# A two-stage MoE kernel on one core: the next unit's first group moved between the last six products of a unit, and the PSUM banks dealt anew

## The chip, the cores and the metric

The kernel runs on one core of one Trainium2 chip. What counts is the device time of one execution in microseconds (us), less is better. Before the change the median of three runs is 2382.3 us (2381.95 to 2382.96).

## The reference, cut to what matters

```python
def _moe2_ref(x, w_gate, w1, w2):          # x (3072, 384): output of attention and a first MoE
    P = np.exp(logits - logits.max())      # logits = x @ w_gate
    for _ in range(8):                     # Sinkhorn
        P /= P.sum(1, keepdims=True) + 1e-09
        P /= P.sum(0, keepdims=True) + 1e-09
        P *= N / E
    for e in range(8):
        h = np.maximum(x @ w1[e], 0.0)     # w1[e] (384, 1024)
        out += P[:, e:e + 1] * (h @ w2[e]) # w2[e] (1024, 384)
```

A delta-rule attention and a first MoE layer come before this; they take the first 947 us or so of the execution and the change doesn't touch them.

## The kernel before, in words

The second MoE is worked off in 24 **units** (e, p): expert e of 8 on the token block p of 3, which is 1024 tokens. Every fp32 product is made of three fp16 matmuls (high by high, high by low, low by high), and both layers use a scheme with seven block products in place of eight.

A unit has two parts. First come four **groups** (class Group, line 1025), k = 0 to 3, for 256 of the 1024 hidden features each. A group has 11 terms, each of three matmuls 128x512 on TensorE (`prod`, L1040). They run in five PSUM banks that the class calls x, y, z, w and v: (0,0) starts in bank x, and its partial sum is copied by ScalarE to banks y, w and z at three places (`fork`, line 1048), where the sum grows on in other directions. From the finished banks ScalarE (`take`) and VectorE (`plus_v`) read c00, c01, c10, c11 and v, and of these come the seven operands of the second layer, A11, A12, A22, S1, S2, S3, S4. Each is rounded to fp16 by ScalarE (`hi`, L1012) and its rest subtracted by VectorE (`lo`, `lo_max`, L1015 and L1018). In the trace they are the tiles h{k}{n}h and h{k}{n}l with n = 0 to 6 in that order: h36l is the low half of S4 of group 3. `head`, `body` and `tail` (lines 1076 to 1114) write a group's operations; S1 to S4 come in `tail`.

Then come four **pairs** (class Pair, line 1118), i = 0 to 3, for 2 x 128 of the block's token rows each. A pair has seven **products** (`product`, L1133) of 12 matmuls 128x192: product 1 reads A11, 2 reads A12, 4 A22, 5 S1, 6 S2, 7 S3 and 3 S4. After each VectorE adds the bank to the sum in SBUF (`put`, line 1155: the rows `acc<-ph` and `acc<-b`). Products 6 and 7 go on in the bank of product 1, product 3 in that of product 5, so 7 of a pair can't start before the put of its 6, nor 3 before the put of 5.

Nothing of this runs in the order in which it is written: `Plan.run` (line 76) deals the operations to the engines, TensorE's in the written order as far as they are ready by its own costs, those of the other engines by due times. The outcome is a fixed queue per engine, and each engine works its queue off in order. The unit loop (lines 1329 to 1378) writes the order: the groups (`head` of group k, `tail` of k - 1, `body` of k), product 1 of pair 0, the last `tail`, the rest of products 1, 2 and 4, and then pair after pair 6, 5, 7, 3 (in the units of expert 0 pair 3 has all its products last, for it shares a bank with pair 0). At the end of a unit come the loads of the next block's x (tiles xoh and xol, `dma`), the stores and loads of the sums, and the weights of coming groups (`weight1`, `weight2`): ScalarE scales and rounds, GpSimd subtracts. In the first two units of expert 0 x is not loaded but made on ScalarE and GpSimd (`operands`). `clear` (line 1321) is a matmul whose result nobody reads; it sets a bank's state so that later matmuls add to what a fork has written there.

## Time and profile before

| | |
|---|---|
| median of three runs | 2382.3 us |
| profiled execution, its own time | 2374.54 us |
| its span, first to last instruction | 2372.8 us, mean granted TensorE clock 0.959 |
| busy over the span: TensorE / VectorE / ScalarE / GpSimd | 2200.5 (93%) / 1702.5 (72%) / 1432.9 (60%) / 680.9 (29%) us |
| second MoE, first to last matmul | 947.2 to 2369.4 us |

The profiled execution is 7.8 us shorter than the median of the runs. A matmul's row gives a modelled end: a 128x192 matmul has a row of 0.25 us, though in a full stream the next one starts 0.083 us later, so rows overlap. "Idle" in brackets at the end of a row is the time in which the engine had no row open just before, and the arrow names the instruction that ended it.

### The profile page before, as it was taken

The page shows a single profiled execution, that of the slowest core. Times are in us where ns is not written, and L with a number is a line of the kernel's source. Part 1 is how long each engine was busy: PE and PEld are TensorE (multiplying, and loading weights), DVE is VectorE, ACT ScalarE, POOL GpSimd, SP SyncE. Part 2 cuts the span into 40 slices and gives each one's busy share as a digit, 9 for nine tenths or more (in the row PEclk, how much of TensorE's full clock was granted, in tenths as well). Part 3 has the DMA queues.
Part 4 walks back from the last instruction along what each step waited for, and adds up shares of the span by engine and source line. Part 5 has one row for each costly group of instructions (what it writes and reads, how often), then busy time and mean ns, then how long its engine had stood idle before and what let it go on. Part 6 is the DMA issues. An engine that isn't in the chain of part 4 may idle for free.

```text
span 2372.8 us, 43674 instructions
## 1 busy us (share of the span) xinstructions
PE 2200.5 (93%) x17324; PEld 1664.1 (70%) x17324; DVE 1702.5 (72%) x3304; ACT 1432.9 (60%) x2632; POOL 680.9 (29%) x748
## 2 busy tenths in 40 slices
PE   6788799999999988989999999999999999999999
PEld 5676677777777766666667677677677677677676
DVE  8567876848574254888677777777777777777777
ACT  6878757465655554666766655655655655656554
POOL 5444402132332254222411421321311312312100
PEclk7678999989999999999999999999999999999999
DMA  3354575545544353323323323323323333323221
GB/s 115 123 187 157 188 264 166 182 157 165 200 150 145 122 211 127 106 76 140 121 101 121 114 101 121 114 101 121 114 100 122 117 109 123 109 103 131 98 102 51
DMA packets 123453, 312.90 MB, mean 132 GB/s; under 512 B 14960, under 2 KB 66800, under 8 KB 117104
## 3 DMA queue, kind: packets, MB, share of 16 engines
q1 hardware_dynamic: 123248, 310.11, 38.2%
q8 instruction: 136, 2.23, 0.4%
q14 instruction: 69, 0.57, 0.1%
HBM read 247.84 MB, written 62.13 MB: 131 GB/s over the span
## 4 chain that ended last, share of the span: by engine, by line
PE 57%; DVE 8%; ACT 2%; POOL 2%; issue 1%; DMA 0%; SPq 0%; DVEq 0%; ACTq 0%; POOLq 0%
PE b L1040 18%; PE ph L1133 13%; PE ph L1040 10%; PE b L1133 10%; PE po L684 1%; PE ph L632 1%; DVE acc L1018 1%; DVE h26l L1015 1%; DVE h36l L1015 1%; DVE c L1018 1%; DVE h35l L1015 1%; DVE h16l L1015 1%; POOL stg L887 0%; DVE gxl L838 0%; POOL w1l L874 0%
## 5 line engine op out<-in xcount | busy, mean ns | idle before, releaser
L1015 POOL TENSOR_TENSOR stg<-stg 128x128 f32<-128x128 f32 (+2 forms) x240 | 157.4, 676 | 900.0 <-ACT stg L1012 896.0
L1040 PEld LDWEIGHTS <-w1h 128*128 128x128 f16 x2112 | 206.2, 98 | 241.6 <-issue 7.9
L1040 PE MATMUL b<-xoh,w1h 128*128 128x512 f16 x672 | 254.7, 379 | 0.0
L1040 PE MATMUL b<-xoh,w1l 128*128 128x512 f16 x672 | 254.7, 379 | 0.0
L1040 PE MATMUL b<-xol,w1h 128*128 128x512 f16 x672 | 254.7, 379 | 0.0
L684 PE MATMUL po<-gh,w 128*128 128x512 f32 (+1 forms) x600 | 221.2, 412 | 11.6 <-ACT gh L672 11.4
L1018 DVE SCALAR_TENSOR_TENSOR acc<-ph,pm,acc 128x192 f32<-128x192 f32 x315 | 134.8, 428 | 134.2 <-PE ph L1133 132.6
L1012 ACT ACTIVATE b<-ph 128x512 f32<-128x512 f32 x288 | 165.9, 584 | 72.6 <-PE ph L1040 66.7
L1040 PEld LDWEIGHTS <-w1l 128*128 128x128 f16 x1056 | 103.4, 98 | 124.6
L632 PE MATMUL ph<-x1h,w 128*128 128x512 f32 (+1 forms) x600 | 184.4, 414 | 4.9 <-DMA w<-wa_scratch 2.9
L1018 DVE SCALAR_TENSOR_TENSOR c<-b,v 128x512 f32<-128x512 f32 x96 | 66.1, 688 | 137.5 <-PE b L1040 131.6
L1012 ACT ACTIVATE v<-b 128x512 f32<-128x512 f32 x96 | 57.1, 595 | 173.6 <-PE b L1040 172.3
L670 DVE TENSOR_TENSOR leak<-leak,ph 128x512 f32<-128x512 f32 (+1 forms) x100 | 66.0, 660 | 117.6 <-ACT leak L669 115.0
L1040 PE MATMUL ph<-xoh,w1h 128*128 128x512 f16 x384 | 145.5, 379 | 4.2 <-ACT b L1012 4.2
L1040 PE MATMUL ph<-xoh,w1l 128*128 128x512 f16 x384 | 145.5, 379 | 0.0
L1040 PE MATMUL ph<-xol,w1h 128*128 128x512 f16 x384 | 145.5, 379 | 0.0
L684 PEld LDWEIGHTS po<-gh,w 128*128 128x128 f32 x600 | 117.3, 198 | 36.9 <-ACT gh L672 16.6
L1012 ACT ACTIVATE c<-b 128x512 f32<-128x512 f32 x192 | 114.3, 595 | 40.7 <-PE b L1040 39.9
L1015 DVE TENSOR_TENSOR c<-c,c 128x512 f32<-128x512 f32 x192 | 134.2, 705 | 1.4
L1018 DVE SCALAR_TENSOR_TENSOR c<-c,c 128x512 f32<-128x512 f32 x192 | 131.6, 698 | 2.0
L684 PE MATMUL po<-gl,w 128*128 128x512 f32 (+1 forms) x300 | 123.9, 414 | 9.5 <-POOL gl L674 6.0
L632 PEld LDWEIGHTS ph<-x1h,w 128*128 128x128 f32 x600 | 113.1, 201 | 27.3 <-DMA w<-wa_scratch 3.3
(433 smaller groups left out, 6924.1 us busy)
## 6 DMA issues: line engine op xcount, KB each, us to landing
w<-wa_scratch SPq DMA_DIRECT2D x100, 768.0 KB, 4.4
acc_scratch<-acc SPq DMA_DIRECT2D x84, 384.0 KB, 2.7
acc<-acc_scratch SPq DMA_DIRECT2D x84, 384.0 KB, 3.7
wraw<-wc SPq DMA_DIRECT2D x128, 192.0 KB, 3.3
stg<-wc SPq DMA_DIRECT2D x64, 384.0 KB, 8.7
xoh<-xo_scratch SPq DMA_DIRECT2D x21, 1152.0 KB, 5.1
xol<-xo_scratch SPq DMA_DIRECT2D x21, 1152.0 KB, 8.2
raw<-wa SPq DMA_DIRECT2D x48, 256.0 KB, 3.0
```

Source lines behind the costliest of these rows:

```text
L632: pe.matmul(out=ps, lhsT=wt[:, c * 128:(c + 1) * 128], rhs=xx[:, c], start=(n == 0), stop=(n == 3 * KD - 1))
L670: dve.tensor_tensor(out=g, in0=g, in1=ps, op=ALU.max)
L684: pe.matmul(out=po[c][:, cols], lhsT=wt[:, DM + c * 128:DM + (c + 1) * 128], rhs=xx, start=(i == 1 and m == 0), stop=(i == n and m == 2), ...
L1012: return vec("ACT", n, lambda e: e.activation(out=out, in_=src, func=func, scale=scale), reads, writes, **kw)
L1015: return vec(eng, n, lambda e: e.tensor_tensor(out=out, in0=a, in1=b, op=fn), reads, writes, **kw)
L1018: return vec("DVE", n, lambda e: e.scalar_tensor_tensor(out=out, in0=a, scalar=scalar, in1=b, op0=f0, op1=f1), reads, writes, **kw)
L1040: ordered(pe.matmul(out=banks[b], lhsT=w[:, a], rhs=x[:, c].rearrange("p s k -> p (s k)"), start=start, stop=i == 2 and (a, c) == terms[-1 ...
L1133: ordered(pe.matmul(out=banks[b][:, 0:HD], lhsT=xx[:, o:o + 128], rhs=wt[:, t], start=first and k == 0 and j == 0, stop=k == NK - 1 and j ...
```

## The change

Six things change in the second MoE. Group 0 of the next unit (`ahead`) is written between the last six products of the present one: its operations stand in `steps`, a generator that stops after each term, and one step is taken after each of these products. That holds for every unit that has a successor with loaded x, 21 of 24; units (0, 0) and (0, 1), whose successor's x is still being made, and the last one have none. Product 6 of all four pairs goes first, then 5, 7 and 3 interleaved over the pairs. Products 5 and 3 get a second bank (`y5`), so that two pairs can be under way. The groups' bank x alternates between 0 and 7 for all experts (before: 7 and 6, and 6 alone for expert 0), y is 1 in place of 2, and v of group 0 is 3. Expert 0's pairs take banks 3 and 4 for y, its pair 3 gets a bank of its own, and the Sinkhorn chain moves from bank 7 to 6; for that two more clears per unit of expert 0 are needed. The puts that begin a sum in expert 0 (`fresh`) move from VectorE to ScalarE. The loads of the next x are written ahead of the products.

```diff
@@ class Group
-                self.x, self.y, self.z, self.w, self.v = 7 - k % 2 if e else 6, 2, 3, 4, 5
+                self.x, self.y, self.z, self.w, self.v = k % 2 * 7, 1, 3, 4, 5 if k else 3
-            def head(self):
+            def steps(self):
                 self.prod(self.x, [(0, 0)])
                 self.fork(self.y)
-
-            def body(self):
+                yield
                 self.prod(self.v, [(7, 7)])
                 self.take("v", self.v)
+                yield
                 self.prod(self.x, [(6, 6)], False)
                 self.fork(self.w)
+                yield
...
@@ class Pair
-                self.x, self.y, self.z = (0, 1, 5, 7 if e else 0)[i], 6, 2
+                self.x, self.y, self.z = (0, 1, 5, 7)[i], 6 if e else 3 + i % 2, 2
+                self.y5 = (6, 2, 6, 2)[i] if e else (3, 4, 2, 2)[i]
-                b = {1: self.x, 6: self.x, 7: self.x, 5: self.y, 3: self.y, 2: self.z, 4: self.y}[n]
+                b = {1: self.x, 6: self.x, 7: self.x, 5: self.y5, 3: self.y5, 2: self.z, 4: self.y}[n]
...
-                    vec("DVE", n, lambda e: e.tensor_copy(out=o, in_=src), [("ps", b)], [("acc", blk)])
+                    copy(n, o, src, [("ps", b)], [("acc", blk)])
...
@@ unit loop
-            if e:
-                order = [(1, 1), (0, 2), (0, 4), (2, 1), (1, 2), (1, 4), (3, 1), (2, 2), (2, 4), (3, 2), (3, 4)]
-            else:
-                order = [(1, 1), (0, 2), (2, 1), (0, 4), (1, 2), (1, 4), (2, 2), (2, 4)]
-            for i, q in order:
-                x[i].product(q)
-            for i, q in [(i, q) for i in range(4 if e else 3) for q in (6, 5, 7, 3)]:
+            if nxt and not made:
+                for i in range(2):
+                    dma(128 * 9 * TB * 2, xo[i].rearrange("p j s k -> p (j s k)"), xo_dram[nxt[1], i],
+                        [("xod", nxt[1], i)], XO if i == 0 else [("xol",)])
+            for i, q in [(1, 1), (0, 2), (0, 4), (2, 1), (1, 2), (1, 4), (3, 1), (2, 2), (2, 4), (3, 2), (3, 4),
+                         (0, 6), (1, 6), (2, 6), (3, 6), (0, 5), (1, 5), (0, 7), (0, 3), (1, 7), (1, 3), (2, 5)]:
                 x[i].product(q)
...
-            if not e:
-                for q in (1, 2, 4, 6, 5, 7, 3):
-                    x[3].product(q)
-            if u + 1 < len(units):
-                clear(2, hb[0][A11][0][:, 0:128], hb[0][A11][0], [("h", 0, A11, 0)])
+            if e == 0:
+                for b in (3, 4):
+                    clear(b, hb[0][S1][0][:, 0:128], hb[0][S1][0], [("h", 0, S1, 0)])
+            if nxt and not made:
+                ahead = Group(*nxt, 0)
+                it = ahead.steps()
+                clear(1, hb[0][S1][0][:, 0:128], hb[0][S1][0], [("h", 0, S1, 0)])
+                next(it)
+            for i, q in ((3, 5), (2, 7), (2, 3), (3, 7), (3, 3)) if e else ((2, 7), (2, 3), (3, 5), (3, 7), (3, 3)):
+                x[i].product(q)
+                if ahead:
+                    next(it)
...
+            for _ in it if ahead else ():
+                pass
             store(e, p, 0)
```

The planner decides where all this ends up. Three places show it.

TensorE in unit (7, 0), at the start of product 7 of pair 0 (it reads h05, S3). Before, the last rows of product 5 (h33, bank ph_10349) stand ahead of it:

```order
L1133 LDWEIGHTS h33h_10318
L1133 MATMUL ph_10349<-w2h1_9564,h33h_10318 128x192
L1133 LDWEIGHTS h33l_10319
L1133 MATMUL ph_10349<-w2h1_9564,h33l_10319 128x192
L1133 LDWEIGHTS h33h_10318
L1133 MATMUL ph_10349<-w2l1_9565,h33h_10318 128x192
L1133 LDWEIGHTS h05h_10280
L1133 MATMUL b0_10343<-w2h4_9570,h05h_10280 128x192
```

Now, product 5 of pair 1 (bank b2_10345) and a term of the next unit's group 0, (7,7) in bank b3, stand ahead of it:

```order
L1139 LDWEIGHTS h33h_10318
L1139 MATMUL b2_10345<-w2l1_9565,h33h_10318 128x192
L1040 LDWEIGHTS w1h3_9558
L1040 MATMUL b3_10346<-xoh_9546,w1h3_9558 128x512
L1040 LDWEIGHTS w1h3_9558
L1040 MATMUL b3_10346<-xol_9547,w1h3_9558 128x512
L1040 LDWEIGHTS w1l3_9559
L1040 MATMUL b3_10346<-xoh_9546,w1l3_9559 128x512
L1139 LDWEIGHTS h05h_10280
L1139 MATMUL b0_10343<-w2h4_9570,h05h_10280 128x192
```

Product 7 of pair 0 was the 17th of its unit's 28 products (12 of kinds 1, 2 and 4, three 6 and one 5 stood ahead) and is now the 19th (12, then four 6 and two 5); in the units with p = 0 of experts 1 to 7 the term (7,7) stands ahead of it as well.

VectorE in the same unit, from h13l (low half of S1, group 1) to the put of product 6 of pair 0 (`acc<-b0`). Before:

```order
L1015 TENSOR_TENSOR h13l_10291<-c111_10336,h13h_10290 128x512
L1015 TENSOR_TENSOR h23l_10305<-c112_10337,h23h_10304 128x512
L1015 TENSOR_TENSOR h33l_10319<-c110_10335,h33h_10318 128x512
L1018 SCALAR_TENSOR_TENSOR acc_10261<-ph_10349,pm_10262,acc_10261 128x192
L1018 SCALAR_TENSOR_TENSOR c101_10333<-c101_10333,c001_10327 128x512
L1018 SCALAR_TENSOR_TENSOR c102_10334<-c102_10334,c002_10328 128x512
L1018 SCALAR_TENSOR_TENSOR c100_10332<-c100_10332,c000_10326 128x512
L1015 TENSOR_TENSOR h15l_10295<-c011_10330,h15h_10294 128x512
L1015 TENSOR_TENSOR h25l_10309<-c012_10331,h25h_10308 128x512
L1015 TENSOR_TENSOR h35l_10323<-c010_10329,h35h_10322 128x512
L1018 SCALAR_TENSOR_TENSOR acc_10261<-b0_10343,pm_10262,acc_10261 128x192
```

Now:

```order
L1015 TENSOR_TENSOR h13l_10291<-c111_10336,h13h_10290 128x512
L1015 TENSOR_TENSOR h23l_10305<-c112_10337,h23h_10304 128x512
L1015 TENSOR_TENSOR h33l_10319<-c110_10335,h33h_10318 128x512
L1018 SCALAR_TENSOR_TENSOR acc_10261<-ph_10349,pm_10262,acc_10261 128x192
L1018 SCALAR_TENSOR_TENSOR acc_10261<-b2_10345,pm_10262,acc_10261 128x192
L1018 SCALAR_TENSOR_TENSOR c101_10333<-c101_10333,c001_10327 128x512
L1018 SCALAR_TENSOR_TENSOR c102_10334<-c102_10334,c002_10328 128x512
L1018 SCALAR_TENSOR_TENSOR c100_10332<-c100_10332,c000_10326 128x512
L1015 TENSOR_TENSOR h15l_10295<-c011_10330,h15h_10294 128x512
L1015 TENSOR_TENSOR h25l_10309<-c012_10331,h25h_10308 128x512
L1015 TENSOR_TENSOR h35l_10323<-c010_10329,h35h_10322 128x512
L1018 SCALAR_TENSOR_TENSOR acc_10261<-b0_10343,pm_10262,acc_10261 128x192
```

VectorE's order here is the same but for one more put ahead of the sums of S4 (c101 to c100).

ScalarE at the end of unit (6, 2), behind h36h (S4 of group 3), where the weights of expert 7 are made (stg is the raw weight, w1h its rounded half; a 128x768 row of w1h reads what GpSimd has added up in stg). Before:

```order
L1012 ACTIVATE stg_10352<-stg_10352,scl_69 128x768
L1012 ACTIVATE w1h4_9560<-stg_10352 128x384
L1012 ACTIVATE stg_10353<-stg_10353,scl_69 128x768
L1012 ACTIVATE w1h0_9552<-stg_10353 128x384
L1012 ACTIVATE w1h4_9560<-stg_10352 128x768
L1012 ACTIVATE stg_10354<-stg_10354,scl_69 128x768
L1012 ACTIVATE w1h1_9554<-stg_10354 128x384
L1012 ACTIVATE stg_10351<-stg_10351,scl_69 128x768
L1012 ACTIVATE w1h0_9552<-stg_10353 128x768
L1012 ACTIVATE v0_10338<-b5_10348 128x512
L1012 ACTIVATE v1_10339<-b5_10348 128x512
```

Now:

```order
L1012 ACTIVATE w1h4_9560<-stg_10352 128x768
L1012 ACTIVATE stg_10354<-stg_10354,scl_69 128x768
L1012 ACTIVATE b1_10344<-b0_10343 128x512
L1012 ACTIVATE w1h1_9554<-stg_10354 128x384
L1012 ACTIVATE v0_10338<-b3_10346 128x512
L1012 ACTIVATE stg_10351<-stg_10351,scl_69 128x768
L1012 ACTIVATE w1h0_9552<-stg_10353 128x768
L1012 ACTIVATE b4_10347<-b0_10343 128x512
L1012 ACTIVATE c000_10326<-b1_10344 128x512
L1012 ACTIVATE h00h_10270<-c000_10326 128x512
L1012 ACTIVATE w1h1_9554<-stg_10354 128x768
L1012 ACTIVATE b3_10346<-b0_10343 128x512
```

The forks of the group ahead (b1, b4 and b3 from b0) now stand between the weight rows, with a row that reads GpSimd's sums ahead of each.

## Rows read from the trace of the kernel before

**Rows 1.** Table of stretches: start:end, length, busy us (instructions) per engine, clock, DMA.
```profile
947.00:2369.00 1422.00, 1374.57 (x11281) 986.78 (x11281) 1099.93 (x2000) 848.84 (x1486) 341.31 (x392) 0.99 0.31 109
1060.30:1063.70 3.40, 3.03 (x20) 2.78 (x20) 2.48 (x8) 1.67 (x3) 3.40 (x4) 0.50 0.00 0
2067.30:2070.70 3.40, 2.97 (x20) 2.74 (x19) 2.61 (x8) 1.31 (x2) 3.32 (x7) 0.50 0.00 0
```
**Rows 2.** Waits view, TensorE, 947 to 2372 us: us in total, times, longest.
```profile
PE ph L1133 <- DVE acc L1018: 17.6, 21, 1.0
PE b L1133 <- DVE acc L1018: 17.4, 8, 2.8
PE ph L1133 <- DVE acc L1164: 6.7, 4, 2.4
PE ph L1040 <- ACT b L1012: 4.2, 6, 1.0
```
**Rows 3.** Waits view, TensorE, 1318 to 2372 us (experts 2 to 7).
```profile
PE ph L1133 <- DVE acc L1018: 15.4, 18, 1.0
PE b L1133 <- DVE acc L1018: 13.1, 6, 2.4
```
**Rows 4.** Timeline, TensorE, unit (5, 0): start, length, instruction, idle before and releaser.
```profile
1871.98 0.25 PE L1133 MATMUL b<-w2h,h00h 128*128 128x192 f16 x1
...
1883.86 0.25 PE L1133 MATMUL b<-w2h,h04h 128*128 128x192 f16 x1
...
1890.42 0.24 PE L1133 MATMUL b<-w2h,h05h 128*128 128x192 f16 x1 [2.44 <-DVE acc L1018]
...
1892.55 0.24 PE L1133 MATMUL ph<-w2h,h06h 128*128 128x192 f16 x1 [0.98 <-DVE acc L1018]
```
**Rows 5.** Timeline, VectorE, the same unit.
```profile
1873.85 0.41 DVE L1018 SCALAR_TENSOR_TENSOR acc<-b,pm,acc 128x192 f32<-128x192 f32 x1
...
1889.36 0.68 DVE L1015 TENSOR_TENSOR h35l<-c,h35h 128x512 f16<-128x512 f32 x1
1889.96 0.41 DVE L1018 SCALAR_TENSOR_TENSOR acc<-b,pm,acc 128x192 f32<-128x192 f32 x1
```
**Rows 6.** Timeline, VectorE, unit (6, 0): its first operation, and h01l.
```profile
2026.06 0.69 DVE L1018 SCALAR_TENSOR_TENSOR c<-b,v 128x512 f32<-128x512 f32 x1 [5.49 <-PE b L1040]
...
2028.21 1.76 DVE L1018 SCALAR_TENSOR_TENSOR h01l<-c,h01h 128x512 f16<-128x512 f32 x1
```
**Rows 7.** Timeline, TensorE: the clears of two units in a row, and a term's first matmul.
```profile
1901.46 0.38 PE L1322 MATMUL b<-h00h 128*128 128x512 f16 x1
1901.67 0.38 PE L1040 MATMUL b<-xoh,w1h 128*128 128x512 f16 x1
...
1958.96 0.38 PE L1322 MATMUL b<-h00h 128*128 128x512 f16 x1
```
**Rows 8.** Timeline, unit (0, 0): ScalarE's scaling of the next x, GpSimd's first and last operations.
```profile
991.22 1.56 ACT L1012 ACTIVATE stg<-stg,scl 128x1536 f32<-128x1536 f32 x1
...
992.92 5.62 POOL L1015 TENSOR_TENSOR stg<-stg 128x256 f32<-128x256 f32 x6 [70.55 <-ACT stg L1012]
...
1004.17 5.59 POOL L1015 TENSOR_TENSOR xol<-stg,xoh 128x256 f16<-128x256 f32 x4
```
**Rows 9.** DMA issues, 1985 to 2015 us: KB each, us from issue to landing.
```profile
xol<-xo_scratch SPq DMA_DIRECT2D x1, 1152.0 KB, 8.9
```
**Rows 10.** Timeline, ScalarE, expert 5: weight rows that waited for GpSimd.
```profile
1894.23 0.84 ACT L1012 ACTIVATE w1h<-stg 128x768 f16<-128x768 f32 x1 [2.73 <-POOL stg L1015]
1898.16 0.68 ACT L1012 ACTIVATE w2h<-stg 128x576 f16<-128x576 f32 x1 [2.51 <-POOL stg L1015]
...
1949.16 0.68 ACT L1012 ACTIVATE w2h<-stg 128x576 f16<-128x576 f32 x1 [2.32 <-POOL stg L1015]
...
2007.50 0.84 ACT L1012 ACTIVATE w1h<-stg 128x768 f16<-128x768 f32 x1 [2.60 <-POOL stg L1015]
...
2011.77 0.84 ACT L1012 ACTIVATE w1h<-stg 128x768 f16<-128x768 f32 x1 [1.22 <-POOL stg L1015]
```

More of the change, by code (lines that the diff above doesn't have):

```diff
@@ L1088, in body @@
                 self.lo(A11, "c00")
+                yield
                 self.prod(self.x, [(5, 5)], False)
                 self.fork(self.z)
+                yield
                 self.prod(self.w, [(3, 8), (4, 3)], False)
@@ L1094, in body @@
                 self.lo_max(A12, "c10")
+                yield
                 self.prod(self.x, [(4, 4)], False)
@@ L1098, in body @@
                 self.lo_max(A22, "c11")
+                yield
             def tail(self):
@@ L1146, in product @@
                 elif n == 5:
-                    self.put(1, HI, self.y, True)
+                    self.put(1, HI, self.y5, True)
                 elif n == 6:
@@ L1152, in product @@
                 else:
-                    self.put(0, HI, self.y)
+                    self.put(0, HI, self.y5)
             def put(self, half, cols, b, fresh=False):
@@ L1257, in sinkhorn @@
             due = [10.0]
-            M = ("ps", 7)
-            mb = banks[7]
+            M = ("ps", 6)
+            mb = banks[6]
             def late():
@@ L1323, in clear @@
                [("ps", b)])
-        for b in (2, 3, 4):
+        for b in (1, 3, 4):
             clear(b, w1o[0][0][:, 0], xo[0][:, 0].rearrange("p s k -> p (s k)"), XO + [("w1", 0)])
@@ L1328, in delta_moe_kernel @@
         units = [(e, p) for e in range(E) for p in range(NT // 2)]
+        ahead = None
         for u, (e, p) in enumerate(units):
@@ L1332, in delta_moe_kernel @@
                     dma(128 * 9 * TB * 2, xo_dram[p, i], xo[i].rearrange("p j s k -> p (j s k)"), XO, [("xod", p, i)])
-            gs = [Group(e, p, k) for k in range(NK)]
+            gs = [ahead] if ahead else [Group(e, p, 0)]
+            gs += [Group(e, p, k) for k in range(1, NK)]
             for k, g in enumerate(gs):
-                g.head()
+                if not ahead or k:
+                    it = g.steps()
+                    next(it)
                 if k:
                     gs[k - 1].tail()
-                g.body()
+                for _ in it:
+                    pass
             if e:
@@ L1341, in delta_moe_kernel @@
                 load(e, p, 2)
+            nxt = units[u + 1] if u + 1 < len(units) else None
+            made = e == 0 and p < 2
             x = [Pair(e, p, i) for i in range(4)]
@@ L1354, in delta_moe_kernel @@
                     mark = [x[0].last]
-            if not e:
-                for q in (1, 2, 4, 6, 5, 7, 3):
-                    x[3].product(q)
-            if u + 1 < len(units):
-                clear(2, hb[0][A11][0][:, 0:128], hb[0][A11][0], [("h", 0, A11, 0)])
-            n = (e + 1) * NK
-            if e == 0 and p < 2:
+            n = (e + 1) * NK
+            ahead = None
+            if e == 0:
[9 more added lines that the diff above has]
+                if ahead:
+                    next(it)
+            if nxt and made:
+                clear(1, hb[0][S1][0][:, 0:128], hb[0][S1][0], [("h", 0, S1, 0)])
                 ss = [load_step(t) for t in (2 * p + 2, 2 * p + 3)]
@@ L1365, in delta_moe_kernel @@
                 (weight1, weight2)[p](n, mark)
-            elif u + 1 < len(units):
-                for i in range(2):
-                    dma(128 * 9 * TB * 2, xo[i].rearrange("p j s k -> p (j s k)"), xo_dram[units[u + 1][1], i],
-                        [("xod", units[u + 1][1], i)], XO if i == 0 else [("xol",)])
+            for _ in it if ahead else ():
+                pass
             store(e, p, 0)
```

## The prediction, made before the changed kernel was run

> **What bounds the kernel now.** I looked at the stretches first, then at who waits for whom, then at single waits in order of time.
>
> The table of stretches shows TensorE busy for 1374.57 us of the 1422 us of the second MoE, VectorE for 1099.93 and ScalarE for 848.84 [rows 1]. So TensorE bounds it, and what can be won is the time in which TensorE waits or runs at half clock. Its floor is in rows too. From the first product of a unit to the thirteenth, 12 products of 12 matmuls, it takes 1883.86 - 1871.98 = 11.88 us [rows 4]: 0.99 us a product, 0.083 us a matmul. A 128x512 matmul starts the next after 0.21 us [rows 7], so a term of three is 0.65 us.
>
> The waits view says what TensorE waits for: 17.6 + 17.4 + 6.7 + 4.2 = 45.9 us in 21 + 8 + 4 + 6 = 39 waits [rows 2], nearly all of a product for a put on VectorE. Each row understates its wait: a matmul's row lasts 0.25 us where the next could start after 0.083 us, which hides 0.16 us. So 39 x 0.16 = 6.2 us come on top, 52.1 us in all. The puts by copy (L1164) and the forks belong to expert 0: 6.7 + 4.2 + 10 x 0.16 = 12.5 us. Of the rest, 15.4 + 13.1 + 24 x 0.16 = 32.3 us lie in experts 2 to 7 [rows 3], and the remaining 7.3 us in expert 1. The 24 waits there are one of about 1 us in each of the 18 units and a second, of up to 2.4 us, in the six with p = 0.
>
> The clock adds to this. The granted clock is 0.99 over the stage and 0.50 (the 1.2 GHz level) in five stretches of 3.40 us; the first and last stand in [rows 1]. Each has some 20 matmuls at 0.17 us instead of 0.083 us, which costs about 1.6 us, 8 us for five. What TensorE did before: ahead of each, within a few us, stand the waits at products 7 and 3. In all **52.1 + 8 = 60.1 us** are there to be won.
>
> Why the wait exists can be read in unit (5, 0), which starts its products at T = 1871.98. Product 7 of pair 0 starts at 1890.42 after an idle row of 2.44 us, product 3 at 1892.55 after 0.98 us, each released by a put [rows 4]. The put of product 6 that frees product 7 is queued on VectorE behind h35l, the low half of S3, and runs at 1889.96, T + 18.0 [rows 5]. VectorE isn't slow there, it is behind: it works without a gap, 0.60 us for one 512-wide operation (h35l at 1889.36 to the next at 1889.96), since the groups ended. It was idle earlier: its first operation of a unit's group comes after 5.49 us of idling for TensorE [rows 6].
>
> **The change part by part.**
>
> *Product 6 first for all pairs.* Nothing is added; TensorE reaches product 7 of pair 0 as the 19th product and not the 17th. In a unit with p = 0 the term (7,7) stands ahead too. So it comes to product 7 at T + 18 x 0.99 + 0.65 = T + 18.5 and to product 3 at T + 19.5. VectorE's order there is the same but for one more put. Unchanged it would end the put of 6 at 1890.37, T + 18.4: the wait at 7 is gone. The put of 5 would come 20.57 - 19.5 = 1.1 us late for product 3.
>
> *Group 0 ahead.* Six terms of the next unit (3.9 us) move between the last six products; two terms (7,7) stood there already, so four (2.6 us) are new there. The first sums on VectorE now come about 1.3 us behind the last product (two terms), where 5.49 us of idling stand before [rows 6]: it starts some 4 us sooner against 2.6 us that TensorE saves. Counted in the order of unit (7, 0), 20 operations and 12 puts lie between the first put and the low half of S4; before it was 23 and 10. That is 3 x 0.60 - 2 x 0.41 = 1.0 us less. So of the 1.1 us some 0.1 us stays. With p = 1 and 2 it is 14 operations where 18 were, 2.4 us less, and product 3 two places later, 2 us: their wait of 1.06 us goes with margin. The work itself costs TensorE nothing: it is the same terms.
>
> *What the early terms need.* The next x must have landed by the first early term, 18 products (17.8 us) behind the last reader of the old x; xol landed 8.9 us after its issue in the worst case that I found [rows 9], and the two loads stand at the same place of the sync engine's queue as before, so about 9 us cover them. The weights of group 0 are made a unit earlier. Forks go through ScalarE's queue, below.
>
> *New banks.* Expert 0's groups alternate between two x banks, so the 4.2 us of forks [rows 2] go. Six clears more at 0.21 us are **1.3 us**, on the path. The 48 puts that go to ScalarE cost it about the 0.41 us of a put each; it is busy 848.84 of 1422 us, and these puts free banks that are asked for two products later. If that cover fails, product 3 of the pair is late by what ScalarE is behind.
>
> *Expert 0's operands.* In units (0, 0) and (0, 1) the next x is made on GpSimd: it began 1.7 us after ScalarE's scaling (991.22 to 992.92) and ended at 1004.17 + 5.59 = 1009.76, a chain of 16.8 us [rows 8]. The scaling now stands behind the put of product 6 of pair 0, the 13th product: the chain runs from about T + 14.6 to T + 31.4. TensorE is through 28 products and three clears at T + 28.4 and has terms for 2 to 3 us that don't need the last part. I take 1.5 us left for each of the two units, 3 us; ends are 0 and 3 us each.
>
> *Sum against the profiled execution (2374.54 us).* Left over are 3 us in expert 0, 2 us in expert 1 (its first unit has eight more ScalarE copies and the longest wait, 2.8 us), 6 x 0.5 = 3 us at p = 0 of experts 2 to 7 (I take 0.5 where 0.1 is worked out; ends 0 and 1.7, the latter if VectorE gains nothing by the early group), one clock drop of five, 1.6 us, and 1.3 us of clears: 10.9 us. The gain is 60.1 - 10.9 = **49.2 us**: 2325.3 us for that execution. The median of the runs is 7.8 us above it for a reason that no row shows; I carry the difference over: 2382.3 - 49.2 = **2333.1 us**. All waits gone would be 60.1 - 1.3 = 58.8 us, 2323.5 us; small waits not in the rows let it reach 2322.
>
> **The rivals.**
>
> *VectorE stays late at p = 0.* There ScalarE and GpSimd make five weights during the groups. The low half h01l took 1.76 us while GpSimd worked, where h35l took 0.68 us [rows 5, 6]: 1.08 us more. If three more of VectorE's operations come to lie beside GpSimd, since they start 4 us sooner, it is 3.2 us later, and product 3 waits 3.3 us: 6 x 3.3 + 5.3 (expert 1) + 8 (all clock drops stay) + 3 + 1.3 = 37.4 us are left, the gain is 22.7 us, **2360 us**. For it: puts, which now fill that time, were not slowed (0.41 us). Against it: GpSimd's rows ran into the groups before the change too. The Trainium skill, SBUF — State Buffer, section Who interferes with whom, says that a VectorE instruction with both inputs in SBUF contends with GpSimd's reads, and one with a single SBUF input doesn't; that would put all early low halves at risk and speaks against this change. By that rule, the trace agrees: the row of 1.76 us shows it, but no row here shows how many of the moved operations meet GpSimd.
>
> *Forks wait behind weights (the other side).* ScalarE works its queue in order, and rows that read GpSimd's sums now stand ahead of forks. Such rows idled 2.73 and 2.51 us in a unit with p = 0, 2.32 with p = 1, 2.60 and 1.22 with p = 2 (expert 5) [rows 10]: 11.4 us per expert, 68.3 us over experts 1 to 6 whose successors' weights are made. If TensorE waits for all of it, the kernel is 68.3 - 49.2 = 19.1 us slower, **2401 us**. It decides from 72% of these waits on (49.2 / 68.3). Against it: the order shows mostly scalings ahead of the first fork, the weight rows begin as soon as S4 is rounded, several us ahead of the first early term, and between (0,0) and the term that needs its fork stand a product and a term, 1.6 us.
>
> *It does nothing.* VectorE would have to be the true bound. It is busy 1099.93 / 24 = 45.8 us of a unit's 57.5 us (1901.46 to 1958.96 [rows 7]); no.
>
> **How the numbers follow.** Forecast 0.70 (its own range 2322 to 2346), VectorE late 0.16, forks late 0.06, no change 0.04; 0.04 is for mixtures between the first two. The range goes from 2322 to 2355, short of the second case's middle, which keeps about three quarters to four fifths. A measurement of this kernel can tell about 0.2% (4.8 us) from no change. Faster by more than that: 0.70 + 0.16 + 0.04 = 0.90; within it 0.04; slower 0.06.
>
> **What would show it right or wrong.** Waits of products for puts in experts 2 to 7 falling from 24 to 6 or fewer, none over 1 us; a unit from clear to clear at 56.4 to 56.5 us, where it was 57.5; VectorE's idle of 5.49 us at the start of a group cut to about 1 us; at most one stretch at 0.50 after 947 us; forks in expert 0 no longer waited for. It is wrong if terms of the early group (L1040) wait for a fork or for x, if h15l to h36l still end behind TensorE at p = 0, or if unit (0, 1) starts its groups with a wait for xol of more than 3 us.

## The result, and the profile after

The changed kernel takes 2322.2 us (median of 4 runs, 2321.3 to 2328.7), the kernel before beside it 2382.1 us (4 runs, 2376.5 to 2383.0): a ratio of 0.977, with a 95% interval of 0.974 to 0.980. That is 60 us less, where 49 us were forecast (2333.1 us, range 2322 to 2355). The time lies 0.2 us inside the lower end of that range.

How much of it is the second MoE? The profiled executions begin it at different times (947.2 us before, 955.8 us after; over all the runs below 946.5 to 956.4), although nothing ahead of it was changed. So I measure each kernel by the stretch from the first clear to the end of the last matmul, 0.25 us more than to that matmul's start: 1422.4 us before, 1367.7 us after, **54.7 us less**. The other 5 us of the medians' difference I put down to the part ahead of it, whose length differs by more than that between profiles; only one execution of each kernel was profiled, so this is not shown.

The table of stretches for the second MoE, which answers [rows 1]: start:end, length, busy us of TensorE, its weight loads, VectorE, ScalarE and GpSimd with their counts, granted clock, DMA share, GB/s.

```profile
955.00:2323.00 1368.00, 1362.20 (x11289) 980.63 (x11289) 1097.78 (x1954) 862.89 (x1535) 342.70 (x392) 1.00 0.32 114
```

TensorE is busy for 1362 of 1368 us, at a clock of 1.00: from 935.8 us to the end no stretch at 0.50 is left. The work of the other engines is what it was; ScalarE has 14 us more (the puts that it took over).

The waits view of TensorE from 945 us on, which answers [rows 2, 3]: us in all, times, longest.

```profile
PE b L1139 <- DVE acc L1018: 1.9, 2, 1.1
PE ph L1139 <- DVE acc L1018: 1.4, 2, 1.0
PE b L1328 <- DVE xmax L690: 1.2, 1, 1.2
PE b L1139 <- DVE acc L1015: 1.0, 1, 1.0
PE b L1139 <- ACT acc L1012: 0.6, 1, 0.6
```

The third row is the first clear, which waits for the end of the first MoE. The first two rows all lie in unit (1, 0), the last two in unit (0, 1). In experts 2 to 7 no product waits at all, where it was 24 times.

I also measured every wait as the time from one matmul's start to the next less the 0.083 us or 0.216 us that it takes, which leaves no 0.16 us hidden. Over 0.12 us, without the router's matmuls, these are some 55.1 us in 48 places before and 6.4 us in 8 after: 48.7 us less. With 1.3 us more of clears, 54.7 - 48.7 + 1.3 = 7.3 us remain for the five stretches at half clock, 1.5 us each.

The unit (5, 0) again, TensorE's timeline, which answers [rows 4]: start, length, instruction. The last two are products 7 and 3 of pair 0.

```profile
1844.20 0.25 PE L1139 MATMUL b<-w2h,h00h 128*128 128x192 f16 x1
...
1862.66 0.25 PE L1139 MATMUL b<-w2h,h05h 128*128 128x192 f16 x1
...
1863.65 0.25 PE L1139 MATMUL ph<-w2h,h06h 128*128 128x192 f16 x1
```

And VectorE in this unit, which answers [rows 5, 6]: its first sum of the unit's first group, then the end of S3 and S4 with the puts of products 6 (at 1861.02) and 5 (at 1863.15) of pair 0.

```profile
1821.09 1.34 DVE L1018 SCALAR_TENSOR_TENSOR c<-b,v 128x512 f32<-128x512 f32 x2 [0.88 <-PE b L1040]
...
1860.42 0.68 DVE L1015 TENSOR_TENSOR h35l<-c,h35h 128x512 f16<-128x512 f32 x1
1861.02 0.41 DVE L1018 SCALAR_TENSOR_TENSOR acc<-b,pm,acc 128x192 f32<-128x192 f32 x1
...
1862.55 0.68 DVE L1015 TENSOR_TENSOR h36l<-c,h36h 128x512 f16<-128x512 f32 x1
1863.15 0.41 DVE L1018 SCALAR_TENSOR_TENSOR acc<-ph,pm,acc 128x192 f32<-128x192 f32 x1
```

The put of 5 ends at 1863.56, and product 3, which goes on in that bank, starts at 1863.65. So the wait is gone by **0.09 us**: next to nothing is to spare at p = 0. Product 7 has 1.2 us to spare.

### The profile page after: what moved, and what is told of

It reads as the page before. It is cut to its first block, busy times and chain, and to the rows that moved or that the text cites. A ratio compares the mean times of both kernels' runs of the same rounds, so it can differ in the third digit from the quotient of the medians.

```text
span 2326.7 us, 43758 instructions
## 1 busy us (share of the span) xinstructions
PE 2197.2 (94%) x17330; PEld 1667.1 (72%) x17330; DVE 1698.8 (73%) x3256; ACT 1446.3 (62%) x2680; POOL 683.1 (29%) x748
## 4 chain that ended last, share of the span: by engine, by line
PE 74%; ACT 10%; DVE 8%; DMA 3%; issue 3%; POOL 3%; SPq 0%; DVEq 0%; POOLq 0%; ACTq 0%
PE b L1040 24%; PE b L1139 18%; PE ph L1139 10%; PE ph L1040 5%; PE ph L632 4%; PE po L684 4%; DMA wraw<-wc 2%; PE y_ps L437 2%; ACT x L362 2%; PE w_ps L428 2%; ACT a_d L296 1%; ACT p L378 1%; PE m_ps L347 1%; ACT u L388 1%; PE g_ps L280 1%
## 5 line engine op out<-in xcount | busy, mean ns | idle before, releaser
L1040 PE MATMUL b<-xoh,w1h 128*128 128x512 f16 x864 | 327.5, 379 | 0.0
L1040 PE MATMUL b<-xoh,w1l 128*128 128x512 f16 x864 | 327.5, 379 | 0.0
L1040 PE MATMUL b<-xol,w1h 128*128 128x512 f16 x864 | 327.5, 379 | 0.0
L1018 DVE SCALAR_TENSOR_TENSOR acc<-b,pm,acc 128x192 f32<-128x192 f32 (+1 forms) x357 | 155.3, 448 | 92.5 <-PE b L1139 91.6
L1012 ACT ACTIVATE b<-b 128x512 f32<-128x512 f32 x144 | 84.1, 584 | 141.1 <-PE b L1040 139.5
L1018 DVE SCALAR_TENSOR_TENSOR acc<-ph,pm,acc 128x192 f32<-128x192 f32 (+1 forms) x231 | 97.9, 432 | 76.9 <-PE ph L1139 76.8
L1018 DVE SCALAR_TENSOR_TENSOR c<-b,v 128x512 f32<-128x512 f32 x144 | 97.5, 689 | 45.9 <-PE b L1040 45.3
L674 POOL TENSOR_TENSOR gl<-leak,gh 128x512 fp32r<-128x512 f32 x48 | 62.2, 1296 | 189.2 <-ACT gh L672 180.5
L669 ACT ACTIVATE leak<-ph 128x512 f32<-128x512 f32 (+1 forms) x100 | 57.7, 577 | 82.1 <-PE ph L632 76.1
L1015 POOL TENSOR_TENSOR w2l<-stg,w2h 128x576 f16<-128x576 f32 (+1 forms) x84 | 94.6, 1149 | 45.7 <-ACT w2h L1012 45.7
```

The source lines that it names most:

```text
L669: act.activation(out=g, in_=ps, func=ACTF.Copy, scale=0.01)
L674: (dve if t in (0, 1, NT - 1) else pool).tensor_tensor(out=gl, in0=g, in1=fr(gh), op=ALU.subtract)
L1012: return vec("ACT", n, lambda e: e.activation(out=out, in_=src, func=func, scale=scale), reads, writes, **kw)
L1015: return vec(eng, n, lambda e: e.tensor_tensor(out=out, in0=a, in1=b, op=fn), reads, writes, **kw)
L1018: return vec("DVE", n, lambda e: e.scalar_tensor_tensor(out=out, in0=a, scalar=scalar, in1=b, op0=f0, op1=f1), reads, writes, **kw)
L1040: ordered(pe.matmul(out=banks[b], lhsT=w[:, a], rhs=x[:, c].rearrange("p s k -> p (s k)"), start=start, stop=i == 2 and (a, c) == terms[-1 ...
```

## The experiments

What each kernel left, from its profiled execution: the second MoE, the waits of TensorE in it as defined above, its time at half clock, and the median of all its runs. The last column can't be compared from row to row: the kernel before, run beside each, had medians of 2382.1 us (changed), 2377.3 us (order_only, early_only, one_bank, late_load), 2379.4 us (before_again, e0_one_x, e0_puts_dve, gp_scale), 2381.7 us (one_bank_no_early, c01_four) and 2376.3 us (five_weights).

| kernel | second MoE us | waits us (places) | half clock us | all runs us |
|---|---|---|---|---|
| before | 1422.4 | 55.1 (48) | 5 x 3.4 | 2382.1 |
| before_again | 1425.1 | 54.8 (48) | 5 x 3.4, 1 x 6.8 | 2385.1, one run |
| changed | 1367.7 | 6.4 (8) | 0 | 2322.2 |
| order_only | 1382.7 | 21.5 (32) | 0 | 2339.9 |
| early_only | 1380.2 | 16.2 (22) | 6.8 | 2337.5 |
| one_bank | 1375.6 | 12.9 (17) | 3.4 | 2327.2 |
| one_bank_no_early | 1377.4 | 15.7 (20) | 0 | 2332.8, one run |
| e0_one_x | 1372.5 | 11.1 (15) | 0 | 2326.8 |
| e0_puts_dve | 1381.0 | 16.7 (11) | 13.7 | 2337.1 |
| late_load | 1367.7 | 6.4 (8) | 0 | 2328.2 |
| gp_scale | 1369.8 | 8.3 (10) | 0 | 2323.5 |
| c01_four | 1369.4 | 8.2 (15) | 0 | 2327.1 |
| five_weights | **1363.8** | 2.5 (4) | 0 | 2316.8 |

**The new order without the early group (order_only).**

```diff
-            if nxt and not made:
-                ahead = Group(*nxt, 0)
-                it = ahead.steps()
...
+            if nxt:
+                clear(1, hb[0][S1][0][:, 0:128], hb[0][S1][0], [("h", 0, S1, 0)])
             if nxt and made:
-                clear(1, hb[0][S1][0][:, 0:128], hb[0][S1][0], [("h", 0, S1, 0)])
```

> The products' new order with the new banks, without the early group: TensorE starts every unit's first group only after the unit's last product, as before the change. Measured by the second MoE, first clear to last matmul: 1422.1 us before, 1367.5 us changed. My theory (the order takes the waits at product 7 and at p = 1 and 2; the head start of the early group is what is needed at p = 0, where product 3 would otherwise come 1.1 us ahead of its put): seven units with p = 0 wait 1.1 us each, unit (1,0) some 2.5 us more, and one clock drop of 1.6 us may come with them: about 1367.5 + 6 x 1.1 + 3.6 + 1.6 = 1379 us, experts 2 to 7 with six waits, all at product 3. Rival 'the order does it all': within 2 us of 1367.5, no waits in experts 2 to 7. Rival 'the early group does it all': 1410 us or more, a wait in each unit.

Measured: 1382.7 us; ratio to before 0.984 (0.983 to 0.986). Its waits view, TensorE:

```profile
PE ph L1139 <- DVE acc L1018: 7.2, 8, 1.0
PE b L1139 <- DVE acc L1018: 4.0, 8, 0.8
PE ph L1040 <- ACT b L1012: 3.2, 12, 0.3
```

At p = 1 and 2 no product waits. At p = 0 of experts 2 to 7 product 7 waits 0.63 us and product 3 1.14 us, 1.8 us a unit where 3.7 us were in all but the first. I had expected the second alone (1379 us). The third row is new: in 12 units a term of the last group, right ahead of the products, waits 0.43 us, hidden part included, for a fork (in unit (2, 2) at 1445.88, 27 us behind the clear).

**The early group with the old order (early_only).** In experts 1 to 7 alone; expert 0 stays as changed.

```diff
...
+            if e:
+                order += [(i, q) for i in range(3) for q in (6, 5, 7, 3)][:-1]
...
-            for i, q in ((3, 5), (2, 7), (2, 3), (3, 7), (3, 3)) if e else ((2, 7), (2, 3), (3, 5), (3, 7), (3, 3)):
+            for i, q in ((2, 3), (3, 6), (3, 5), (3, 7), (3, 3)) if e else ((2, 7), (2, 3), (3, 5), (3, 7), (3, 3)):
```

> The early group with the new banks, but in experts 1 to 7 the products of a pair in the old order 6, 5, 7, 3, pair by pair. My theory (the early group gives VectorE 1.0 us at p = 0 and 2.4 us at p = 1 and 2): the waits at p = 1 and 2, about 1 us, go; at p = 0 the waits at products 7 and 3, 2.4 + 1.0 us, shrink to about 2.4 us together; unit (1,0) waits some 3 us more than now and two or three clock drops come back. Second MoE: 1367.5 + 6 x 2.4 + 3 + 4 = 1389 us, 1382 to 1396. Rival 'the early group does it all': within 2 us of 1367.5. Rival 'the order does it all': 1410 us or more, with a wait at product 7 in every unit.

Measured: 1380.2 us, just below the expected range; ratio 0.983 (0.981 to 0.985). The waits at p = 1 and 2 are gone but for one of 0.23 us, and at p = 0 there remain 0.15 + 1.14 us. So either half alone clears p = 1 and 2, and both are needed at p = 0. Against before, order_only is 39.7 us shorter, early_only 42.2 and the changed kernel 54.7. Each of these holds what expert 0's own changes bring, which stay in all three: some 12 us (from the first clear to the last product of expert 0 it is 191.3 us before, 182.7 us in early_only and in the changed kernel, and these two have 3.9 us of early terms in it). In experts 1 to 7 the halves alone thus bring some 27 and 30 us, together 42: they overlap.

Unit (1, 0) of this kernel shows what the clock does. TensorE's timeline, the rows that waited, and the table of stretches behind them:

```profile
1176.48 0.24 PE L1139 MATMUL b<-w2h,h05h 128*128 128x192 f16 x1 [2.11 <-DVE acc L1018]
1178.61 0.32 PE L1139 MATMUL ph<-w2h,h06h 128*128 128x192 f16 x1 [0.98 <-DVE acc L1018]
```
```profile
1177.70:1184.50 6.80, 5.89 (x38) 5.41 (x38) 3.52 (x9) 1.76 (x3) 6.64 (x10) 0.50 0.01 2
```

The wait of 2.11 us ends at 1176.48; from 1177.7 on the granted clock is 0.50, the 1.2 GHz level, for 6.8 us. This kernel's second MoE is 12.5 us longer than the changed kernel's and its waits are 9.8 us more: the other 2.7 us I put down to the clock.

**The kernel before once more (before_again).**

> The kernel before, unchanged, profiled a second time: do the stretches at half clock stand at the same waits? My theory (a drop follows a place where TensorE has just waited 3 us or more in two waits close together): each drop behind product 3 of pair 0 of a unit with p = 0 or behind the waits of expert 0, none elsewhere, four to seven in all; which of those eight or so places have one may differ. Rival (the drops come by themselves, evenly in time): drops at other units too, behind single waits of about 1 us or none.

Measured: six stretches at half clock, at 1068.5, 1198.2, 1546.4, 1723.9, 1901.3 and 2252.9 us. All begin at the end of a wait of 2.4 us or more (from start to start) at product 7, or of one as long in unit (0, 1), or within 2.1 us behind it; so do four of the five of the first profile, and the one at 1060.3 us began 0.4 us before such a wait ended (2.49 us, to 1060.67). One of them, the rows that waited ahead of it and the stretch:

```profile
1545.57 0.24 PE L1133 MATMUL b<-w2h,h05h 128*128 128x192 f16 x1 [2.44 <-DVE acc L1018]
1547.70 0.32 PE L1133 MATMUL ph<-w2h,h06h 128*128 128x192 f16 x1 [0.77 <-DVE acc L1018]
```
```profile
1546.40:1553.20 6.80, 6.03 (x39) 5.50 (x38) 3.49 (x9) 1.66 (x3) 6.72 (x10) 0.50 0.01 2
```

My condition "behind two waits close together" is too narrow: the stretch began before the second. Which of the like places has one differs between the profiles (1901.3 and 2252.9 only in this one, 2067.3 only in the first), so a long wait makes a drop likely and not certain. The rival is out: in these two profiles no drop stands anywhere else.

**One bank for products 5 and 3 (one_bank), and that without the early group (one_bank_no_early).** The order of experts 1 to 7 has product 5 of a pair behind product 3 of the pair before; the second kernel also has the edit of order_only.

```diff
-                self.y5 = (6, 2, 6, 2)[i] if e else (3, 4, 2, 2)[i]
+                self.y5 = 6 if e else (3, 4, 2, 2)[i]
...
+                order += [(0, 6), (1, 6), (2, 6), (3, 6), (0, 5), (0, 7), (0, 3), (1, 5), (1, 7), (1, 3), (2, 5)]
...
-            for i, q in ((3, 5), (2, 7), (2, 3), (3, 7), (3, 3)) if e else ((2, 7), (2, 3), (3, 5), (3, 7), (3, 3)):
+            for i, q in ((2, 7), (2, 3), (3, 5), (3, 7), (3, 3)):
```

> Early group and products of S2 first, but in experts 1 to 7 products 5 and 3 of every pair share one bank, as before the change, so product 5 of a pair has to stand behind product 3 of the pair before and follows it at once. My theory (a put needs about 0.6 us from the end of its product to the release of its bank, and the second bank is what lets the two halves of the order go on without it): three such places a unit, 0.6 us each, in 21 units, 38 us: second MoE 1405 us, 1395 to 1415, with waits at product 5 of pairs 1 to 3 and none at 7; the clock may drop again, up to 8 us. Rival 'the second bank is not needed': 1367 to 1372 us.

Measured: 1375.6 us, 30 us better than expected. Three waits of 0.67 us, the price of a put that I had put at 0.6, stand in the last unit, which has no early group behind it, and in no other; at p = 0 of experts 2 to 7 product 3 waits 0.63 us. The rest of the difference to the changed kernel is unit (1, 0) and one drop. I had not thought of the planner: it lets a later TensorE operation go first where its costs say that the next in the program isn't ready. It set products 7 of other pairs and terms of the early group between products that share the bank.

> One bank for products 5 and 3 in experts 1 to 7, S2's products first, and no early group. With the early group one bank cost 7.9 us, not the 38 I expected: products 7 went between, and ahead of the last three products terms of the early group. My theory now (three waits of 0.67 us for a put stand at the end of each unit, as in the last one, wherever no early term fills them): the second MoE of the run with the order only, 1382.7 us, plus 20 units x 2.0 us, 1423 us. Rival (the terms weren't what hid them; the order of products alone did): 1383 to 1392 us.

Measured: 1377.4 us, so the theory that I had formed falls too, and for the same reason. TensorE's timeline at the end of unit (5, 0): the clear that the program has ahead of the next unit's groups, a term, product 3 of a pair, three terms, and product 5 of the last pair.

```profile
1869.01 0.38 PE L1328 MATMUL b<-h03h 128*128 128x512 f16 x1
1869.22 0.38 PE L1040 MATMUL b<-xoh,w1h 128*128 128x512 f16 x1
...
1869.87 0.25 PE L1139 MATMUL ph<-w2h,h06h 128*128 128x192 f16 x1
...
1870.86 0.38 PE L1040 MATMUL b<-xoh,w1h 128*128 128x512 f16 x1
...
1872.81 0.25 PE L1139 MATMUL ph<-w2h,h03h 128*128 128x192 f16 x1
```

The clear and seven terms of the next unit run ahead of this unit's last product, though the program has all of them behind: with one bank the planner sees the waits and draws the next unit's terms forward, and so makes most of the early group itself. In the three units of expert 5, 18 terms of the next unit run ahead of the last product here, 18 in the changed kernel and one in order_only. This kernel is 5.3 us faster than order_only, which has the bank more. As I read it, the planner foresees no wait in order_only and draws less forward, and VectorE is then late by what its costs leave out; no run tests this by itself. So the second bank for product 5, with the order that goes with it, is worth 7.9 us in experts 1 to 7 beside the early group; without the early group the kernel that has it is the slower one. 38 us was wrong.

**Expert 0: one x bank (e0_one_x), and puts on VectorE (e0_puts_dve).**

```diff
-                self.x, self.y, self.z, self.w, self.v = k % 2 * 7, 1, 3, 4, 5 if k else 3
+                self.x, self.y, self.z, self.w, self.v = k % 2 * 7 if e else 7, 1, 3, 4, 5 if k else 3
```

> Expert 0 only: all four groups of a unit use one x bank again (bank 7), where the change alternates two; all else as changed. My theory (the next group's first term waits until the old x has been read, 0.83 to 1.21 us at six places before the change): about 0.8 us at two of three changes of group in each of three units, 5 us: second MoE 1372.5 us. Rival (the new order of the terms covers it): 1367.7 us, no wait of a term of more than 0.3 us.

Measured: 1372.5 us, as expected, with this row in its waits view:

```profile
PE ph L1040 <- ACT b L1012: 4.0, 5, 1.0
```

```diff
-                    copy(n, o, src, [("ps", b)], [("acc", blk)])
+                    vec("DVE", n, lambda e: e.tensor_copy(out=o, in_=src), [("ps", b)], [("acc", blk)])
```

> Expert 0 only: the 48 puts that were moved to ScalarE go back to VectorE; all else as changed. Expert 0 waits 0.3 + 0.3 + 0.7 + 1.2 = 2.5 us now and about 15 us before. My theory (VectorE has the router's small operations beside the groups in units (0,0) and (0,1), so the puts must leave it): waits at product 3 of about 2.5 us come back in these two units, 0.5 us in the third: second MoE 1367.7 + 5 = 1373 us, with a clock drop perhaps 1375. Rival (the order and the banks alone are enough in expert 0): 1366.5 to 1368 us; the 0.7 us that TensorE now waits for a put on ScalarE would go.

Measured: 1381.0 us, a miss in size: 13.3 us more than the changed kernel, not 5 to 7. The waits of unit (0, 1), and the clock behind the first of them:

```profile
1064.07 0.32 PE L1139 MATMUL b<-w2h,h05h 128*128 128x192 f16 x1 [5.15 <-DVE acc L1170]
```
```profile
1061.10:1074.70 13.60, 7.21 (x45) 6.55 (x45) 11.32 (x21) 5.60 (x9) 11.29 (x10) 0.50 0.32 116
```

Product 7 waits 5.3 us there and a later product 3.7 us, more than at any place before the change, and the clock is at 0.50 for 13.7 us. So the move of the puts to ScalarE is no trifle beside the rest: to undo it costs 13.3 us, to leave out the early group 15.0 us and the new order of the products, in experts 1 to 7, 12.5 us.

**What is left in unit (1, 0): late_load, gp_scale, c01_four, five_weights.** 3.9 us of the 6.4 us stand there. First I suspected ScalarE's eight scalings of the accumulator, which only expert 1 has.

```diff
                 load(e, p, 0)
+            if e > 1:
                 load(e, p, 2)
...
             gs[-1].tail()
+            if e == 1:
+                load(e, p, 2)
```

> Expert 1 only: the load of the accumulator's second half (pairs 2 and 3), with its four scaling copies on ScalarE, goes behind the last group's second part, where it stood ahead of the products. Unit (1,0) now waits 1.23 + 0.54 + 0.95 + 1.14 = 3.9 us at products 2, 2, 7 and 3. My theory (ScalarE works eight scaling copies of 0.6 us ahead of the roundings of S1 to S4 and of the scaled halves that the first puts need): four fewer ahead give 2.4 us of ScalarE's time, and 2 to 3 us of the 3.9 go: second MoE 1365 us. Rival (VectorE is what is late in that unit, by the low halves beside GpSimd): no change, 1367.5 us. Rival (the copies then stand ahead of puts of pairs 2 and 3): waits move to product 4 of pair 2, 1368 us or more.

Measured: 1367.7 us, the same waits. This tests nothing: the planner sorts by due times, and the order on every engine came out as it was.

```diff
-                        copy(DM, acc[:, j], acc[:, j], [("acc", j), ("pm",)], [("acc", j)], scale=pm[:, t, 0:1])
+                        tensor(DM, acc[:, j], acc[:, j], pm[:, t, 0:1].to_broadcast([128, DM]), ALU.mult,
+                               [("acc", j), ("pm",)], [("acc", j)], "POOL")
```

> Expert 1 only: the 24 scaling operations of the loaded accumulator go from ScalarE to GpSimd (a product with the gate broadcast along the row), which idles 25 us in unit (1,0) from its groups on. That unit now waits 1.23 + 0.54 + 0.95 + 1.14 = 3.9 us. My theory (six scalings stand on ScalarE ahead of the last group's c01 and of its roundings, and hold VectorE up): the waits shrink to about 1 us, second MoE 1365 us. Rival (GpSimd is slower, about 1 us for a 128x384 product, and the puts of pair 0 then wait for it; VectorE's low halves beside it also take longer): 1369 us or more.

Measured: 1369.8 us. The four waits stay as they were, and two of 0.98 us are added, for h22l and h32l. The rival's time came out (1369 us or more), and the low halves that take longer show in the timeline: GpSimd's rows, then VectorE's at the same time. Because the edit gives GpSimd more work, this run alone doesn't clear ScalarE's scalings.

```profile
1156.80 4.65 POOL L1015 TENSOR_TENSOR w2l<-stg,w2h 128x576 f16<-128x576 f32 x3
1161.42 3.74 POOL L1015 TENSOR_TENSOR acc<-acc,pm 128x384 f32<-128x384 f32 x3
```
```profile
1158.77 1.54 DVE L1015 TENSOR_TENSOR h30l<-c,h30h 128x512 f16<-128x512 f32 x1
1160.23 0.68 DVE L1018 SCALAR_TENSOR_TENSOR c<-ph,v 128x512 f32<-128x512 f32 x1
1160.83 1.17 DVE L1018 SCALAR_TENSOR_TENSOR h31l<-c,h31h 128x512 f16<-128x512 f32 x1
1161.93 1.31 DVE L1018 SCALAR_TENSOR_TENSOR h12l<-c,h12h 128x512 f16<-128x512 f32 x1
1163.16 1.31 DVE L1018 SCALAR_TENSOR_TENSOR h22l<-c,h22h 128x512 f16<-128x512 f32 x1
1164.39 1.31 DVE L1018 SCALAR_TENSOR_TENSOR h32l<-c,h32h 128x512 f16<-128x512 f32 x1
```

While GpSimd works, an operation with both inputs in SBUF takes 1.17 to 1.54 us in place of 0.68, and the one that reads PSUM (`c<-ph,v`) keeps its 0.68. The Trainium skill, SBUF — State Buffer, section Who interferes with whom, says that a VectorE instruction with two inputs in SBUF contends with GpSimd instructions that read SBUF, and one with at most one such input, in the plain modes (a limit that the prediction left out), doesn't; the rows agree.

In that trace c01 of the last group also waited for h05l, which reads the buffer that it takes over. Hence a fourth buffer:

```diff
-              for n, m in (("c00", 3), ("c01", 3), ("c10", 3), ("c11", 3), ("v", 2))}
+              for n, m in (("c00", 3), ("c01", 4), ("c10", 3), ("c11", 3), ("v", 2))}
```

> The changed kernel with a fourth buffer for c01 (one more 128x512 tile), so that the last group of a unit doesn't take over the one that the first group's h05l still has to read. In unit (1,0) c01 of the last group was seen to wait for that h05l, with ScalarE idle 5.2 us ahead of it where GpSimd did the scalings. My theory (this reuse, not ScalarE's scalings, starts the last group's chain of sums 3 us late in that unit): the waits of 3.9 us there fall to 1 to 2 us, second MoE 1365.5 us, nothing changes in experts 2 to 7. Rival (VectorE is simply behind by that much work in unit (1,0), in whatever order): 1367.7 us, the same waits.

Measured: 1369.4 us. The waits of unit (1, 0) add up to 4.1 us, spread otherwise, so they don't come from the buffer; and product 3 now waits 0.15 us in each p = 0 unit of experts 2 to 7, where it had 0.09 us to spare. A miss.

The last suspect was GpSimd: unit (0, 2) makes six weight tiles for expert 1, a unit of the later experts' five.

```diff
                 (weight1, weight2)[p](n, mark)
+                if p:
+                    weight2(n + 1, mark)
...
-                    if e == 0:
-                        weight2(n + 1, mark)
```

> One of the six weight tiles that unit (0,2) makes for expert 1 is made in unit (0,1) instead; the later experts make five there. In unit (1,0) and ahead of it GpSimd is busy 35.2 us of 65, in the like stretch of expert 2 28.6 us of 59, and VectorE's operations with both inputs in SBUF take 1.1 to 1.8 us beside it, where they take 0.68 alone. My theory (the sixth weight is what puts VectorE and ScalarE behind in unit (1,0)): the 3.9 us of waits there fall to below 1.5 us, second MoE 1364.5 to 1366 us, nothing else changes. Rival (the eight scalings and the accumulator's load leave VectorE behind whatever GpSimd does): 3 to 4 us of waits stay in unit (1,0), 1367 to 1368 us; more than that if unit (0,1), which waits 2.2 us now, takes the work badly.

Measured: 1363.8 us, just below the 1364.5 to 1366 expected and 3.9 us less than the changed kernel, with no wait left in unit (1, 0); ratio to before 0.974 (0.971 to 0.978). Its waits view in full:

```profile
PE b L1328 <- DVE xmax L690: 1.2, 1, 1.2
PE b L1139 <- DVE acc L1015: 1.0, 1, 1.0
PE b L1139 <- ACT acc L1012: 0.6, 1, 0.6
```

So the sixth tile was the cause: without it no wait is left, and ScalarE's eight scalings, which stayed, don't bring one by themselves. By its profiled stretch it is the best version of this study. Whole runs don't tell it from the changed kernel: beside the kernel before it gains 59.6 us (2376.3 to 2316.8 us) where the changed kernel gained 59.9 us. What the tile takes away, GpSimd's beside VectorE or ScalarE's own four operations on it, was not told apart.

## Why the prediction was right, and where its terms were off

- **What bounds it, and what was to be won.** Right: TensorE, 60.1 us of waits and half clock by rows; by starts of matmuls it is 55.1 + 7.3 = 62.4 us. "Without a gap" was not quite so: VectorE idled 0.36 us once among the products of unit (5, 0), at 1878.12.
- **Product 6 first.** TensorE's side is right to a tenth of a us: product 7 at 1862.66, T + 18.46 (said: 18.5), product 3 at T + 19.45 (19.5). order_only shows this half alone: the waits at p = 1 and 2 go, but at p = 0 1.8 us stay where this step says 1.1, and product 7, whose wait it calls gone, still waits 0.63 us. The step leaves out the put that now stands ahead on VectorE (0.33 us from its start to the next row's), which the next step counts; the other 0.3 us or so stay open.
- **Group 0 ahead.** Right: VectorE's idling at a group's start fell from 5.49 us to 0.88, and the put of 6 runs at T + 16.8, 1.2 us sooner than before (said: 1.0). A put takes 0.33 us of VectorE's time and not the 0.41 us of its row, so the counted operations give 3 x 0.60 - 2 x 0.33 = 1.1 us, and "some 0.1 us stays" came out as 0.09 us to spare. I had then taken 0.5 us a unit to be careful: 3 us too much.
- **From unit to unit** it is 56.43 us (unit (2, 0) starts its products at 1336.37, (5, 0) at 1844.20, nine units), as forecast.
- **Clock.** I left one stretch of five; none is left: 1.6 us too much. The price of 1.6 us for one was right (1.5 us). That they go with the waits is what before_again, early_only and one_bank show: every drop stands at one of their longer waits.
- **Expert 0.** Size right (3 us said, 2.5 us found), mechanism half: the operand chain holds no term of the next unit up. The ScalarE put that product 3 waits 0.7 us for in unit (0, 1) stands behind a rounding of these operands that itself idled 2.5 us for GpSimd, the failed cover that I had named for the new banks and priced at nothing:

```profile
1071.84 1.06 ACT L1012 ACTIVATE xoh<-stg 128x1024 f16<-128x1024 f32 x1 [2.53 <-POOL stg L1015]
1072.80 0.31 ACT L1012 ACTIVATE acc<-b 128x192 f32<-128x192 f32 x1
```

- **Expert 1.** The term that was too small: 2 us said, 3.9 us found. I gave ScalarE's eight scalings as the reason. five_weights left them there, took one weight tile away, and the waits went; gp_scale moved them to GpSimd, and the waits stayed.
- **New banks.** 4.2 us for the forks of expert 0 were forecast, 4.8 us found (e0_one_x). The puts on ScalarE I had called covered, with no gain of their own; e0_puts_dve gives them 13.3 us.
- **Left over:** 10.9 us said (3 + 2 + 3 + 1.6 + 1.3), 6.4 + 1.3 = 7.7 us found. So the gain is 62.4 - 7.7 = 54.7 us in place of 60.1 - 10.9 = 49.2. Of the 10.9 us between 2333.1 and 2322.2, 5.5 us are this; the other 5.4 us lie outside the second MoE: I had carried over the 7.8 us by which the profiled execution was shorter than the median, for which no row gave a reason, and the part ahead differs by up to 9.9 us between profiles. That the time fell inside the range is in part luck: 2322.2 lies below the 2323.5 us that I gave for all waits gone, although 7.7 us are left, and only 0.2 us above the lower end of the range.
- **Rivals.** *VectorE late at p = 0*: contention with GpSimd is there (h10l took 1.76 us in unit (5, 0)), but no more of it than before: VectorE's 512-wide rows in the groups of that unit exceed 0.69 us each by some 3.2 us in all, where it was 3.5. Some operations got away: h01l of unit (6, 0) went from 1.76 us [rows 6] to 0.69. With 0.09 us to spare it was close. *Forks behind weights*: no term waits for a fork after expert 0. *Does nothing*: no, the interval of the ratio ends at 0.980.

What stays open: the 1.2 us of unit (0, 1) at a put on VectorE (the other 0.7 us there is told above), and how the sixth tile acts.

## What to carry to other kernels

When a product waits for a bank, look when the engine that empties it began: moving the consumer later in its own engine's order and starting that engine sooner gave some 27 and 30 us alone and 42 us together in experts 1 to 7 here, and only both together cleared the tightest units. Where a planner sets the order, a written order is a wish: compare what the engines ran before a result is put down to an edit (late_load changed nothing, one_bank_no_early rebuilt most of the group that it left out). Weigh a unit that still waits against a like one that doesn't, and look first at what it has more of on the engines off the path: here one weight tile in six was 3.9 us.

## What was not expected of the hardware

In one place half clock lasted 13.7 us (e0_puts_dve, from 1061.1 us on), around two waits of 5.3 and 3.7 us; the other drops, at waits of 1.6 to 2.9 us, lasted 3.4 or 6.8 us. One place doesn't make this a rule. The drop began 3 us before the first of the two waits ended. In that stretch TensorE was busy 7.2 of 13.6 us, so the drop cost less than its length: of the kernel's 13.3 us 10.3 us are waits, and the other 3 us I put down to the clock.
